# Whole K loads, w_out's remainder in four transfers, and mask copies on GpSimd in a decode step bound by its cache reads

## The chip, the cores and the metric

The kernel runs on one core of one Trainium2 chip. The core has five engines with instruction streams of their own: TensorE (PE; its weight loads are listed as PEld), VectorE (DVE), ScalarE (ACT), GpSimd (POOL) and SyncE (SP), which here only issues transfers. Sixteen DMA engines move data between the memory outside (HBM) and the on-chip SBUF. The metric is the device time of one execution in microseconds, as the median of several runs.

## The reference

One decode step of attention with a large cache, and a small gated MLP beside it, both on the layer-normed input (weights, caches and inputs in bfloat16):

```python
# x (4,1,640); k_cache, v_cache (4,32,4096,128); wq (640,4096); wo (4096,640)
# w_in (640,1728); w_sp (1,1); b_sp (1,); w_out (864,640)
xn = layernorm(x)
# A: attention of 4 x 32 heads, one query each
q = (xn @ wq) as (4,32,1,128)
p = softmax(q . k_cache * 128**-0.5)          # over 4096 keys
A = (p . v_cache) as (4,1,4096) @ wo
# B: gated MLP
z  = gelu_tanh(xn @ w_in)                     # (4,1,1728)
z2 = layernorm(z[..., 864:])
g  = w_sp * z2 + b_sp
B  = (z[..., :864] * g) @ w_out
out = x + A + B
```

Each cache holds 134 MB, and every byte of it is used once. The other weights come to some 14 MB.

## The kernel before

**Units and places.** The caches are cut into 16 units each: 4 groups g of 8 heads, times 4 batch rows b, with u = 4g + b. A unit is 8.39 MB, 65536 bytes on each of 128 partitions. The SBUF has five slots of half a unit; every load has a fixed pair of them. A K load of an odd unit goes to slots 2 and 3, of an even one to 3 and 4, and a V load mostly to 0 and 1. SyncE issues the loads in the order of `seq`, and each issue waits until the last reader of its slots is done.

```python
    seq = [("k", u) for u in range(B)]
    for u in range(NU):
        seq.append(("v", u))
        if u + B < NU:
            seq.append(("k", u + B))
    ...
    for u in range(B, NU):
        place[("k", u)] = (3, 4) if u % 2 == 0 else (2, 3)
    for u in range(NU):
        place[("v", u)] = (0, 1)
    place[("v", 0)] = (1, 2)
    place[("v", NU - 3)] = (2, 3)
    place[("v", NU - 1)] = (3, 4)
    cuts = {("k", u): (0, T // 2, T) for u in range(NU) if u % B == B - 1}
    cuts[("v", NU - 1)] = (0, 192, T)
    first = {u: u % 2 for u in range(B, NU) if ("k", u) not in cuts}
    ...
        for t0, t1 in zip(c[:-1], c[1:]):
            nc.sync.dma_start(out=unit(item, t0, t1), in_=src[:, t0 * Dh:t1 * Dh])
```

A load in `cuts` comes as two transfers, each with its own completion: the last K of each group (units 3, 7, 11 and 15). `first` says which half of a whole K load is read first, so that the slot which the next K load needs comes free early.

**K side.** A unit of K takes eight steps. In each, VectorE transposes 128 x 2048 words into one of two `kT` buffers, and TensorE multiplies that with the queries (QZ) into the scores S of the group.

```python
        hh = first.get(u, 0) ^ (k // 4)
        ...
        kT = ktpool.tile([P, NKT], F32, tag="kT", name="kT")[:, 0:2 * TC * 32]
        nc.vector.transpose(kT[:].rearrange("p (t r) -> p t r", r=32), kw)
        ...   # 8 matmuls of 128x512
```

After the group's fourth unit the softmax follows: maximum, exponent (ScalarE), a transpose, sixteen copies into `xd`, and then the masks for b = 0 and 1. `z_fill` writes the weights of TensorE's V side into one of two buffers Zb, each head masked by MkE:

```python
    def z_fill(g, b):
        xd = state[("xd", g)]
        for hp in range(HP):                  # 4
            ...
            for e in range(NE):               # 2
                dst = Zb[b % 2][r0:r0 + 32, :, NE * hp + e, :]
                mk = MkE[r0:r0 + 32, e:e + 1]
                if b == 0 and e == 0 and hp < 3:
                    nc.vector.tensor_scalar(out=dst, in0=src, scalar1=mk, scalar2=None, op0=ALU.mult)
                else:
                    nc.scalar.activation(out=dst, in_=src, func=ACT.Copy, scale=mk)
```

**V side.** A unit of V is 64 matmuls with Zb as weights. VectorE then masks and sums the result, and the masks for b + 2 are written.

```python
        for w in range(NW):
            q = w % 4
            nc.tensor.matmul(O_ps[32 * q:32 * q + 32, :, :], lhsT=Zb[b % 2][:, w].rearrange("p h c -> p (h c)"),
                             rhs=vv[:, w * 4 * Dh:(w + 1) * 4 * Dh], start=(w < 4), stop=(w >= NW - 4))
        ...
        if b + 2 < B:
            z_fill(g, b + 2)
```

**MLP.** Its 864 inner columns are 512 on all partitions (FA = 4 chunks) and a remainder of 352, laid out as 44 partitions x 8 chunks. `w_rest` holds the rows of w_out for the remainder and borrows one of the two `kT` buffers before the first K unit needs it:

```python
    w_rest_t = ktpool.tile([P, NKT], F32, tag="kT", name="w_rest")
    w_rest = w_rest_t[:NRP].bitcast(BF16)[:, 0:FR * NOUT].rearrange("p (c n) -> p c n", c=FR)
    r_at = [nf, nf + FR * RP[0], Fh]
    for i in range(2):
        nc.sync.dma_start(out=w_rest[32 * i:32 * i + RP[i]].rearrange("p c n -> p (c n)"),
                          in_=B_w_out[r_at[i]:r_at[i + 1], :].rearrange("(r i c) n -> i r (c n)", r=4, c=FR))
```

The first transfer has i = 8 by r = 4 rows of 10240 bytes, the second i = 3 by r = 4.

Of the kernel before, what the change touches and what calls it, by code (L numbers as in the profile page):

```python
# [9 lines left out]
ALU = mybir.AluOpType  # L10
AX = mybir.AxisListType
F32 = mybir.dt.float32
BF16 = mybir.dt.bfloat16
# [3 lines left out]
def kernel(  # L17
# [19 lines left out]
    nc = tc.nc  # L37
    P = 128
    B, Sq, D = A_x.shape
    _, H, Sk, Dh = A_k_cache.shape  # L40
    assert Sq == 1 and B == 4 and Dh == P and D % P == 0
    DC = D // P
# [4 lines left out]
    T = Sk // M  # L47
    C2 = 2
    TC = 32
# [3 lines left out]
    NU = NG * B  # L53
    G = HG * B
    F2 = B_w_in.shape[1]
    Fh = F2 // 2
    FA = 4
    FR = 8
    RI = (8, 3)
    RP = [4 * i for i in RI]  # L60
    NRP = sum(RP)
    assert Fh == FA * P + FR * NRP and RP[0] == 32
    FC = FA + FR
    NOUT = A_wo.shape[1]
    NH = 2
    NO2 = NOUT // NH
# [3 lines left out]
    const = ctx.enter_context(tc.tile_pool(name="const", bufs=1))  # L70
    small = ctx.enter_context(tc.tile_pool(name="small", bufs=2))

    NKT = max(2 * TC * 32, FR * NOUT // 2)
    ktpool = ctx.enter_context(tc.tile_pool(name="ktpool", bufs=2))
    ppool = ctx.enter_context(tc.tile_pool(name="ppool", bufs=3))
    ps_s = ctx.enter_context(tc.tile_pool(name="ps_s", bufs=1, space=bass.MemoryType.PSUM))
# [7 lines left out]
    def misc_ps(shape, dtype):  # L84
        misc_ctr[0] += 1
        return ps_m.tile(shape, dtype, tag="misc", name=f"misc{misc_ctr[0]}")
# [5 lines left out]
    def at_slot(i, n, off=0):  # L92
        return kv[:, i * SL + off:i * SL + off + n]
# [24 lines left out]
    nf = FA * P  # L118
    w_out = at_slot(2, FA * NOUT, n_in).rearrange("p (c n) -> p c n", c=FA)
    nc.sync.dma_start(out=w_out, in_=B_w_out[0:nf, :].rearrange("(p c) n -> p c n", p=P))  # L120
    w_rest_t = ktpool.tile([P, NKT], F32, tag="kT", name="w_rest")
    w_rest = w_rest_t[:NRP].bitcast(BF16)[:, 0:FR * NOUT].rearrange("p (c n) -> p c n", c=FR)
    r_at = [nf, nf + FR * RP[0], Fh]
    for i in range(2):
        nc.sync.dma_start(out=w_rest[32 * i:32 * i + RP[i]].rearrange("p c n -> p (c n)"),  # L125
                          in_=B_w_out[r_at[i]:r_at[i + 1], :].rearrange("(r i c) n -> i r (c n)", r=4, c=FR))

    NB = 32 * FC
    z_at = n_in + FA * NOUT
# [12 lines left out]
    place[("v", 0)] = (1, 2)  # L142
    place[("v", NU - 3)] = (2, 3)
    place[("v", NU - 1)] = (3, 4)
    cuts = {("k", u): (0, T // 2, T) for u in range(NU) if u % B == B - 1}
    cuts[("v", NU - 1)] = (0, 192, T)
    first = {u: u % 2 for u in range(B, NU) if ("k", u) not in cuts}

    def unit(item, t0, t1):

        s0, s1 = place[item]
        assert s1 == s0 + 1 or t1 <= T // 2 or t0 >= T // 2
        if t0 >= T // 2:
            return at_slot(s1, (t1 - t0) * Dh, t0 * Dh - SL)
        return at_slot(s0, (t1 - t0) * Dh, t0 * Dh)
# [50 lines left out]
    xnT = const.tile([P, DC, 32], BF16)  # L206
# [67 lines left out]
    for hf in range(2):  # L274
        for c in range(DC):
            for j in range(NG):
                n0 = j * HG * Dh + hf * 512
                nc.tensor.matmul(q4_ps[32 * j:32 * j + 32, hf * 512:hf * 512 + 512], lhsT=xnT[:, c, :],  # L278
                                 rhs=wq[:, c, n0:n0 + 512], start=(c == 0), stop=(c == DC - 1))
# [13 lines left out]

    w_z = w_in.rearrange("p c (a f) -> p c a f", a=2)
    z_ps = misc_ps([P, 2, FA, 32], F32)
    zr_ps = misc_ps([64, 2, FR * 32], F32)
    w_za = w_z[:, :, :, 0:nf].rearrange("p c a (q j i) -> p c q a i j", q=4, j=32)
    for c in range(DC):
        for q in range(4):
            nc.tensor.matmul(z_ps[32 * q:32 * q + 32], lhsT=xnT[:, c, :], rhs=w_za[:, c, q], start=(c == 0), stop=(c == DC - 1))  # L300
        for i in range(2):
            nc.tensor.matmul(zr_ps[32 * i:32 * i + 32, :, 0:FR * RP[i]], lhsT=xnT[:, c, :],
                             rhs=w_z[:, c, :, r_at[i]:r_at[i + 1]], start=(c == 0), stop=(c == DC - 1))
    z_f = at_slot(2, 2 * 3 * NB, z_at).bitcast(F32).rearrange("p (a n) -> p a n", a=3)
    z_b = at_slot(2, 2 * NB, z_at + 6 * NB).rearrange("p (a n) -> p a n", a=2)
    zT = z_f[:, 0:2, :].rearrange("p a (i j) -> p a i j", j=32)
    nc.gpsimd.memset(z_f[:, 0:2, :], 0.0)
    nc.scalar.activation(out=zT[:, :, 0:FA, :], in_=z_ps[:], func=ACT.Gelu_apprx_tanh)
    for i in range(2):
        for a in range(2):  # L310
            nc.scalar.activation(out=zT[32 * i:32 * i + 32, a, FA:FC, 0:RP[i]].rearrange("p c (i r) -> p c i r", r=4),
                                 in_=zr_ps[32 * i:32 * i + 32, a, 0:FR * RP[i]].rearrange("p (r i c) -> p c i r", r=4, c=FR),
                                 func=ACT.Gelu_apprx_tanh)

    one_bf = const.tile([1, P], BF16)
# [19 lines left out]
                                   op0=ALU.mult, op1=ALU.subtract)  # L335
# [14 lines left out]
    for fc in range(FC):  # L350
        n = P if fc < FA else NRP
        nb = B if fc > 1 else 32
        r0 = 64 * (fc % 2)
        for hf in range(NH):
            nc.tensor.matmul(proj[r0 + 32 * hf:r0 + 32 * hf + nb, 0:NO2], lhsT=uT[:n, fc, 0:nb],
                             rhs=(w_out[:, fc] if fc < FA else w_rest[:, fc - FA])[:, hf * NO2:(hf + 1) * NO2], start=(fc < 2), stop=False)


    def fill_qz(g):
# [8 lines left out]
    def emit_K(u, k):  # L368
# [5 lines left out]
        kw = unit(("k", u), t0, t0 + 2 * TC).bitcast(F32).rearrange("p (t w) -> p t w", w=KW)[:, :, 32 * kh:32 * kh + 32]  # L374
        kT = ktpool.tile([P, NKT], F32, tag="kT", name="kT")[:, 0:2 * TC * 32]
        nc.vector.transpose(kT[:].rearrange("p (t r) -> p t r", r=32), kw)  # L376
# [34 lines left out]
    def z_fill(g, b):  # L411
        xd = state[("xd", g)]
        for hp in range(HP):
            r0 = 32 * hp
            src = xd[r0:r0 + 32, C2 * b:C2 * b + C2].rearrange("p x q (y c) -> p (x q y) c", c=4)
            for e in range(NE):
                dst = Zb[b % 2][r0:r0 + 32, :, NE * hp + e, :]
                mk = MkE[r0:r0 + 32, e:e + 1]
                if b == 0 and e == 0 and hp < 3:
                    nc.vector.tensor_scalar(out=dst, in0=src, scalar1=mk, scalar2=None, op0=ALU.mult)  # L420
                else:
                    nc.scalar.activation(out=dst, in_=src, func=ACT.Copy, scale=mk)  # L422

    def softmax(g):
        negmax = softmax_max(g)
        S_ps = state.pop(("S", g))
        p_bf = ppool.tile([P, TC, NE, M], BF16, tag="p", name="p")
        rowsum = small.tile([P, NE], F32, tag="rowsum")
        for e in range(NE):
            nc.scalar.activation(out=p_bf[:, :, e, :], in_=S_ps[:, e], func=ACT.Exp, bias=negmax[:, e:e + 1], scale=scale,  # L430
                                 accum_out=rowsum[:, e:e + 1])

        pT = ppool.tile([P, TC, HP, B * C2], BF16, tag="p", name="pT")
        nc.vector.transpose(pT[:].rearrange("p t h x -> p (t h x)"), p_bf[:].rearrange("p t e m -> p (t e m)"))  # L434

        xd = small.tile([P, B * C2, 4, TC], BF16, tag="xd", name="xd", bufs=1)
        state[("xd", g)] = xd
        for hp in range(HP):
            for q in range(4):
                op = nc.vector.tensor_copy if q < 2 or (hp < 3 and q == 2) else nc.scalar.copy  # L440
                op(out=xd[32 * hp:32 * hp + 32, :, q, :], in_=pT[32 * q:32 * q + 32, :, hp, :].rearrange("p t x -> p x t"))  # L441
        z_fill(g, 0)
        z_fill(g, 1)
        rs8 = small.tile([P, NE, B], F32, tag="rs8")
        nc.gpsimd.tensor_tensor(out=rs8[:], in0=rowsum[:, :, None].to_broadcast((P, NE, B)),  # L445
                                in1=MkB[:, None, :].to_broadcast((P, NE, B)), op=ALU.mult)
        cs = misc_ps([P, B], F32)
        for e in range(NE):
            nc.tensor.matmul(cs[:], lhsT=SelE[:, e].rearrange("p h e q -> p (h e q)"), rhs=rs8[:, e, :],  # L449
                             start=(e == 0), stop=(e == NE - 1))  # L450
        rinv = small.tile([P, B], F32, tag="rinv")
        nc.vector.reciprocal(out=rinv[:], in_=cs[:])
        state[("rinv", g)] = rinv
# [56 lines left out]
    for i, item in enumerate(seq):  # L510
        if i + 1 < len(seq):
            key, u = seq[i + 1]
# [10 lines left out]
        key, u = item  # L523
        g, b = divmod(u, B)
# [31 lines left out]
    for c in range(HG):  # L556

        p = part.get(c, 0)
        lhsT = oT[:, c, :] if p in seen else oT[:, c:c + HG, :].rearrange("p c b -> p (c b)")
        nb = B if p in seen else 32  # L560
        for hf in range(NH):
            nc.tensor.matmul(last[p][32 * hf:32 * hf + nb, :], lhsT=lhsT,  # L562
                             rhs=wo_t[NG - 1][:, c, hf * NO2:(hf + 1) * NO2], start=p not in seen, stop=c in (5, HG - 1))
# [36 lines left out]
```

## Time and profile before

| | |
|---|---|
| time, median of 3 runs | 663.5 us (663.31 to 663.76) |
| span of the profiled execution | 661.7 us |
| DVE busy | 362.1 us (55%), 282.8 of it in the K transposes (L376, 128 of 2276 ns) |
| PE busy | 289.6 us (44%) |
| ACT busy | 78.8 us (12%), 52.9 of it in 116 mask copies (L422, 498 ns each) |
| POOL busy | 21.1 us (3%) |
| read from HBM | 282.25 MB, mean 427 GB/s over the span |

The page's numbered parts are the busy time of the engines, the span in 40 slices of 16.5 us each (a digit is the busy share in tenths), the DMA queues, the chain of work that ended last, the costliest groups of instructions and the transfers. L376 and the like are lines of the kernel. Engine names with a q at the end (SPq) stand for that engine's issuing part. A line of the timeline gives the start, the duration, the engine, the line and operation, the tiles written and read with their shapes, the number of instructions in a row, and in brackets the idle time before them with what ended it. The trace also has each DMA packet with its start, duration and size, but not the number of its DMA engine. A transfer over all sixteen DMA engines reports sixteen completions, one for each engine; where they come apart, the engines are at different points of the same queue.

### The profile page before, as it was taken

To read this page: it belongs to the slowest core of one execution; us is meant where nothing else is said; L and a number is where in the kernel's file an instruction comes from. 1 tells how busy PE (TensorE), PEld (TensorE's weight loads), DVE (VectorE), ACT (ScalarE), POOL (GpSimd) and SP (SyncE) were. 2 spreads that over 40 slices of the span, in tenths; PEclk is the share of its full clock that TensorE was granted. 3 is DMA by queue.
4 is the path that set the end of the run, shared out by engine and by line. 5 is a ranking of instruction groups with operands and counts; after the bars stand their busy time and mean duration, and the time that the engine had idled before them with its cause. 6 is when DMAs were issued, how large, how long until landed. Compare 5 with 4: busy or idle time off the path is not lost.

```text
span 661.7 us, 5325 instructions
## 1 busy us (share of the span) xinstructions
PE 289.6 (44%) x2246; PEld 105.5 (16%) x2246; DVE 362.1 (55%) x279; ACT 78.8 (12%) x165; POOL 21.1 (3%) x66
## 2 busy tenths in 40 slices
PE   0425655356072455224436065533707255533235
PEld 0101111112021122111112021110202112111112
DVE  2238999656191759619256286745529175961113
ACT  0300000430100000530200000070020000053200
POOL 6300000000000000000000000000000000000000
PEclk9859979779577687677758587765767758766677
DMA  9999999999999999999999999999999999999996
GB/s 373 450 445 420 424 447 442 420 445 421 436 433 436 428 419 451 421 436 445 436 420 437 420 425 450 443 428 433 416 444 433 440 425 418 435 444 426 427 423 273
DMA packets 6891, 282.59 MB, mean 427 GB/s; under 512 B 787, under 2 KB 1063, under 8 KB 1447
## 3 DMA queue, kind: packets, MB, share of 16 engines
q1 hardware_dynamic: 6847, 282.25, 98.9%
q8 instruction: 17, 0.28, 0.2%
q14 instruction: 7, 0.06, 0.0%
q10 hardware_dynamic: 20, 0.01, 0.0%
HBM read 282.25 MB, written 0.01 MB: 427 GB/s over the span
## 4 chain that ended last, share of the span: by engine, by line
DMA 73%; DVE 11%; issue 11%; PE 2%; ACT 1%; SPq 1%; DVEq 0%; ACTq 0%
DMA kv<-in_A_k_cache_dram 65%; DVE kT L376 11%; DMA kv<-in_A_v_cache_dram 5%; DMA kv<-in_A_wo_dram 3%; PE O L461 1%; ACT Zb L422 0%; ACT xd L441 0%; SPq L125 0%; ACT p L430 0%; DVE pT L434 0%; PE last_a L562 0%; DVE m L394 0%; PE S L387 0%; SPq L172 0%; PE misc L399 0%
## 5 line engine op out<-in xcount | busy, mean ns | idle before, releaser
L376 DVE STREAM_TRANSPOSE kT<-kv 128x2048 f32<-128x2048 f32 x128 | 282.8, 2276 | 121.8 <-DMA kv<-in_A_k_cache_dram 121.7
L387 PE MATMUL S<-kT,QZ 128*32 128x512 bf16 x1024 | 188.0, 500 | 256.7 <-DVE kT L376 256.7
L387 PEld LDWEIGHTS <-QZ 128*32 128x32 bf16 x1024 | 60.0, 110 | 382.6 <-issue 323.5
L461 PE MATMUL O<-kv,Zb 128*32 128x512 bf16 x1024 | 76.7, 466 | 59.0 <-DMA kv<-in_A_v_cache_dram 41.9
L470 DVE TENSOR_TENSOR om<-O,Mk 128x512 f32<-128x512 f32 x15 | 10.4, 692 | 111.2 <-PE O L461 111.2
L422 ACT ACTIVATE Zb<-xd,MkE 32x256 bf16<-32x256 bf16 x116 | 52.9, 498 | 113.5 <-PE O L461 112.1
L430 ACT ACTIVATE p<-S,negmax 128x512 bf16<-128x512 f32 x8 | 5.4, 683 | 400.0 <-DVE negmax L408 400.0
L461 PEld LDWEIGHTS <-Zb 128*32 128x32 bf16 x1024 | 33.7, 115 | 102.8 <-issue 66.3
L362 POOL COPY QZ<-qT 32x32 bf16<-32x32 bf16 x16 | 5.1, 317 | 383.3 <-PE S L387 382.7
L441 DVE COPY xd<-pT 32x256 bf16<-32x256 bf16 x44 | 15.9, 361 | 0.8
L471 DVE TENSOR_REDUCE R<-om 128x128 f32<-128x512 f32 x15 | 15.3, 1019 | 0.5
L441 ACT COPY xd<-pT 32x256 bf16<-32x256 bf16 x20 | 12.3, 613 | 5.6 <-DVE pT L434 5.2
L449 PE MATMUL misc<-rs,SelE 128*128 128x4 f32 x16 | 4.1, 359 | 11.4 <-POOL rs L445 8.5
L434 DVE STREAM_TRANSPOSE pT<-p 128x1024 bf16<-128x1024 bf16 x4 | 5.0, 1245 | 6.3 <-ACT p L430 6.3
L473 DVE TENSOR_SCALAR R<-O,Mk 128x128 f32<-128x128 f32 x1 | 0.4, 351 | 14.0 <-PE O L461 14.0
L278 PE MATMUL q<-kv,xnT 128*32 128x512 bf16 x40 | 4.5, 630 | 7.6 <-DMA kv<-in_A_wq_dram 7.6
L483 PE MATMUL misc<-R,SelX 128*128 128x512 f32 x8 | 4.5, 644 | 7.2 <-DVE R L471 5.5
L394 DVE TENSOR_REDUCE m<-S 128x2 f32<-128x1024 f32 x4 | 4.9, 1225 | 4.9 <-PE S L387 4.9
L286 DVE CAST kv<-q 128x512 bf16<-128x512 f32 x1 | 0.7, 692 | 11.8 <-PE q L278 11.8
L399 PE MATMUL misc<-dg,ones_f 128*128 128x256 f32 x8 | 3.1, 474 | 7.2 <-DVE dg L396 7.2
L445 POOL TENSOR_TENSOR rs<-rowsum,MkB 128x8 f32<-128x8 f32 x4 | 0.8, 201 | 166.4 <-ACT p L430 166.4
L449 PEld LDWEIGHTS misc<-rs,SelE 128*128 128x128 f32 x16 | 3.7, 322 | 13.3 <-POOL rs L445 9.7
(103 smaller groups left out, 76.1 us busy)
## 6 DMA issues: line engine op xcount, KB each, us to landing
kv<-in_A_k_cache_dram SPq DMA_DIRECT2D x8, 4096.0 KB, 29.8
kv<-in_A_v_cache_dram SPq DMA_DIRECT2D x1, 6144.0 KB
kv<-in_A_wq_dram SPq DMA_DIRECT2D x1, 5120.0 KB, 15.1
kv<-in_A_wo_dram SPq DMA_DIRECT2D x3, 1280.0 KB, 21.5
kv<-in_B_w_in_dram SPq DMA_DIRECT2D x1, 2160.0 KB
kv<-in_A_v_cache_dram SPq DMA_DIRECT2D x1, 2048.0 KB
kv<-in_B_w_out_dram SPq DMA_DIRECT2D x1, 640.0 KB, 20.8
kv<-in_A_wo_dram SPq DMA_DIRECT2D x1, 640.0 KB
```

The source lines that it names most:

```text
L362: nc.gpsimd.tensor_copy(out=QZ[r0:r0 + 32, :, :, :, 8 + 8 * hp], in_=qT[32 * g:32 * g + 32, NE * hp:NE * hp + NE].rearrange("p e a b -> p ...
L376: nc.vector.transpose(kT[:].rearrange("p (t r) -> p t r", r=32), kw)
L387: nc.tensor.matmul(S_ps[32 * q:32 * q + 32, e], lhsT=QZ[:, b, 2 * kh + w, e, w0:w0 + 32], rhs=kb[:, i, :, e, :, w], start=(b == 0 and k < ...
L394: nc.vector.tensor_reduce(out=m1[:], in_=S_ps[:].rearrange("p e t m -> p e (t m)"), axis=AX.X, op=ALU.max)
L422: nc.scalar.activation(out=dst, in_=src, func=ACT.Copy, scale=mk)
L430: nc.scalar.activation(out=p_bf[:, :, e, :], in_=S_ps[:, e], func=ACT.Exp, bias=negmax[:, e:e + 1], scale=scale, accum_out=rowsum[:, e:e + 1])
L434: nc.vector.transpose(pT[:].rearrange("p t h x -> p (t h x)"), p_bf[:].rearrange("p t e m -> p (t e m)"))
L441: op(out=xd[32 * hp:32 * hp + 32, :, q, :], in_=pT[32 * q:32 * q + 32, :, hp, :].rearrange("p t x -> p x t"))
L449: nc.tensor.matmul(cs[:], lhsT=SelE[:, e].rearrange("p h e q -> p (h e q)"), rhs=rs8[:, e, :], start=(e == 0), stop=(e == NE - 1))
L461: nc.tensor.matmul(O_ps[32 * q:32 * q + 32, :, :], lhsT=Zb[b % 2][:, w].rearrange("p h c -> p (h c)"), rhs=vv[:, w * 4 * Dh:(w + 1) * 4 * ...
L470: nc.vector.tensor_tensor(out=om4[:], in0=O_ps[:], in1=Mk4[:, :, None].to_broadcast((P, 4, Dh)), op=ALU.mult)
L471: nc.vector.tensor_reduce(out=R, in_=om4[:].rearrange("p c d -> p d c"), axis=AX.X, op=ALU.add)
```

## The change

It has three parts:

- The last K loads of the second and third group (units 7 and 11) come whole. Their halves are then read in the order that `first` gives: slot 3 first, which the next K load needs. The last K loads of the first and the fourth group (units 3 and 15) stay cut in two. This makes for fewer transfers with longer rows.
- The remainder of w_out is laid out as 44 partitions x 9 chunks, of which the last two are partly filled: four transfers of 8 x 4 rows of 8960 bytes, 5 x 4 of 1280, 3 x 4 of 8960 and 3 x 4 of 2560. Seven chunks lie in one `kT` buffer and two in the other, so both are borrowed, and the `kT` buffers shrink from 10240 to 8960 bytes per partition. GpSimd clears the second buffer first. The GELU of the remainder comes in eight pieces instead of four.
- For b = 2 and 3, half of the mask copies (hp = 2 and 3, four of eight) go to GpSimd: 32 of the 128 copies, which relieves ScalarE.

The order of instructions on TensorE and VectorE is otherwise kept: in both kernels the selection and sum of the group before (L486 to L494) stand ahead of the eight transposes of the group's last K unit.

```diff
@@ -55,11 +55,10 @@
     F2 = B_w_in.shape[1]
     Fh = F2 // 2
     FA = 4
-    FR = 8
-    RI = (8, 3)
-    RP = [4 * i for i in RI]
-    NRP = sum(RP)
-    assert Fh == FA * P + FR * NRP and RP[0] == 32
+    FR = 9
+    RB = ((0, 0, 8, 7), (0, 7, 5, 1), (1, 0, 3, 7), (1, 7, 3, 2))
+    NRP = 44
+    assert Fh == FA * P + 4 * sum(i * c for _, _, i, c in RB)
     FC = FA + FR
     NOUT = A_wo.shape[1]
     NH = 2
@@ -70,7 +69,7 @@
     const = ctx.enter_context(tc.tile_pool(name="const", bufs=1))
     small = ctx.enter_context(tc.tile_pool(name="small", bufs=2))
 
-    NKT = max(2 * TC * 32, FR * NOUT // 2)
+    NKT = max(2 * TC * 32, 7 * NOUT // 2)
     ktpool = ctx.enter_context(tc.tile_pool(name="ktpool", bufs=2))
     ppool = ctx.enter_context(tc.tile_pool(name="ppool", bufs=3))
     ps_s = ctx.enter_context(tc.tile_pool(name="ps_s", bufs=1, space=bass.MemoryType.PSUM))
@@ -118,12 +117,17 @@
     nf = FA * P
     w_out = at_slot(2, FA * NOUT, n_in).rearrange("p (c n) -> p c n", c=FA)
     nc.sync.dma_start(out=w_out, in_=B_w_out[0:nf, :].rearrange("(p c) n -> p c n", p=P))
-    w_rest_t = ktpool.tile([P, NKT], F32, tag="kT", name="w_rest")
-    w_rest = w_rest_t[:NRP].bitcast(BF16)[:, 0:FR * NOUT].rearrange("p (c n) -> p c n", c=FR)
-    r_at = [nf, nf + FR * RP[0], Fh]
-    for i in range(2):
-        nc.sync.dma_start(out=w_rest[32 * i:32 * i + RP[i]].rearrange("p c n -> p (c n)"),
-                          in_=B_w_out[r_at[i]:r_at[i + 1], :].rearrange("(r i c) n -> i r (c n)", r=4, c=FR))
+    w_rest = []
+    for k, n in ((0, 7), (1, 2)):
+        t = ktpool.tile([P, NKT], F32, tag="kT", name=f"w_rest{k}")[:NRP].bitcast(BF16)[:, 0:n * NOUT]
+        w_rest.append(t.rearrange("p (c n) -> p c n", c=n))
+    nc.gpsimd.memset(w_rest[1].rearrange("p c n -> p (c n)").bitcast(F32), 0.0)
+    r_at = [nf]
+    for q, c0, ni, n in RB:
+        r_at.append(r_at[-1] + 4 * ni * n)
+        k = c0 // 7
+        nc.sync.dma_start(out=w_rest[k][32 * q:32 * q + 4 * ni, 0:n].rearrange("p c n -> p (c n)"),
+                          in_=B_w_out[r_at[-2]:r_at[-1], :].rearrange("(r i c) n -> i r (c n)", r=4, c=n))
 
     NB = 32 * FC
     z_at = n_in + FA * NOUT
@@ -142,7 +146,7 @@
     place[("v", 0)] = (1, 2)
     place[("v", NU - 3)] = (2, 3)
     place[("v", NU - 1)] = (3, 4)
-    cuts = {("k", u): (0, T // 2, T) for u in range(NU) if u % B == B - 1}
+    cuts = {("k", u): (0, T // 2, T) for u in (B - 1, NU - 1)}
     cuts[("v", NU - 1)] = (0, 192, T)
     first = {u: u % 2 for u in range(B, NU) if ("k", u) not in cuts}
 
@@ -293,23 +297,25 @@
 
     w_z = w_in.rearrange("p c (a f) -> p c a f", a=2)
     z_ps = misc_ps([P, 2, FA, 32], F32)
-    zr_ps = misc_ps([64, 2, FR * 32], F32)
+    zr_ps = misc_ps([64, 2, 256], F32)
     w_za = w_z[:, :, :, 0:nf].rearrange("p c a (q j i) -> p c q a i j", q=4, j=32)
     for c in range(DC):
         for q in range(4):
             nc.tensor.matmul(z_ps[32 * q:32 * q + 32], lhsT=xnT[:, c, :], rhs=w_za[:, c, q], start=(c == 0), stop=(c == DC - 1))
-        for i in range(2):
-            nc.tensor.matmul(zr_ps[32 * i:32 * i + 32, :, 0:FR * RP[i]], lhsT=xnT[:, c, :],
-                             rhs=w_z[:, c, :, r_at[i]:r_at[i + 1]], start=(c == 0), stop=(c == DC - 1))
+        for q in range(2):
+            f0, f1 = r_at[2 * q], r_at[2 * q + 2]
+            nc.tensor.matmul(zr_ps[32 * q:32 * q + 32, :, 0:f1 - f0], lhsT=xnT[:, c, :],
+                             rhs=w_z[:, c, :, f0:f1], start=(c == 0), stop=(c == DC - 1))
     z_f = at_slot(2, 2 * 3 * NB, z_at).bitcast(F32).rearrange("p (a n) -> p a n", a=3)
     z_b = at_slot(2, 2 * NB, z_at + 6 * NB).rearrange("p (a n) -> p a n", a=2)
     zT = z_f[:, 0:2, :].rearrange("p a (i j) -> p a i j", j=32)
     nc.gpsimd.memset(z_f[:, 0:2, :], 0.0)
     nc.scalar.activation(out=zT[:, :, 0:FA, :], in_=z_ps[:], func=ACT.Gelu_apprx_tanh)
-    for i in range(2):
+    for (q, c0, ni, n), f0, f1 in zip(RB, r_at[:-1], r_at[1:]):
+        f0, f1 = f0 - r_at[2 * q], f1 - r_at[2 * q]
         for a in range(2):
-            nc.scalar.activation(out=zT[32 * i:32 * i + 32, a, FA:FC, 0:RP[i]].rearrange("p c (i r) -> p c i r", r=4),
-                                 in_=zr_ps[32 * i:32 * i + 32, a, 0:FR * RP[i]].rearrange("p (r i c) -> p c i r", r=4, c=FR),
+            nc.scalar.activation(out=zT[32 * q:32 * q + 32, a, FA + c0:FA + c0 + n, 0:4 * ni].rearrange("p c (i r) -> p c i r", r=4),
+                                 in_=zr_ps[32 * q:32 * q + 32, a, f0:f1].rearrange("p (r i c) -> p c i r", r=4, c=n),
                                  func=ACT.Gelu_apprx_tanh)
 
     one_bf = const.tile([1, P], BF16)
@@ -353,7 +359,7 @@
         r0 = 64 * (fc % 2)
         for hf in range(NH):
             nc.tensor.matmul(proj[r0 + 32 * hf:r0 + 32 * hf + nb, 0:NO2], lhsT=uT[:n, fc, 0:nb],
-                             rhs=(w_out[:, fc] if fc < FA else w_rest[:, fc - FA])[:, hf * NO2:(hf + 1) * NO2], start=(fc < 2), stop=False)
+                             rhs=(w_out[:, fc] if fc < FA else w_rest[(fc - FA) // 7][:, (fc - FA) % 7])[:, hf * NO2:(hf + 1) * NO2], start=(fc < 2), stop=False)
 
 
     def fill_qz(g):
@@ -418,6 +424,8 @@
                 mk = MkE[r0:r0 + 32, e:e + 1]
                 if b == 0 and e == 0 and hp < 3:
                     nc.vector.tensor_scalar(out=dst, in0=src, scalar1=mk, scalar2=None, op0=ALU.mult)
+                elif b > 1 and hp > 1:
+                    nc.gpsimd.tensor_scalar(out=dst, in0=src, scalar1=mk, scalar2=None, op0=ALU.mult)
                 else:
                     nc.scalar.activation(out=dst, in_=src, func=ACT.Copy, scale=mk)
```

## The prediction

> **What bounds the kernel now.** I read the page's slices first, then the DMA queues, then the chain that ended last, and only then the engines.
>
> ```profile
> DMA  9999999999999999999999999999999999999996
> GB/s 373 450 445 420 424 447 442 420 445 421 436 433 436 428 419 451 421 436 445 436 420 437 420 425 450 443 428 433 416 444 433 440 425 418 435 444 426 427 423 273
> ...
> q1 hardware_dynamic: 6847, 282.25, 98.9%
> ...
> DMA 73%; DVE 11%; issue 11%; PE 2%; ACT 1%; SPq 1%; DVEq 0%; ACTq 0%
> ```
>
> All but the last slice have the DMA engines at nine tenths or more, and SyncE's queue fills 98.9% of sixteen engines' span. No compute engine passes 55%. So the time is 282 MB at the engines' own rate, plus the head, the tail and any bubble; an edit counts only if it alters (a) the time of the packets, (b) their spread over the sixteen engines, or (c) lets an engine run dry because a load was issued too late. In the packet records a 65536-byte packet takes 2424 ns (27.0 GB/s an engine, 433 GB/s for sixteen), a 32768-byte one 1217.6 ns. The chain's 11% of VectorE is hidden time: each DMA link in it lasts about 29.8 us although 8.39 MB needs 19.4; the rest is queueing behind the load before.
>
> For (c) I looked for the load with the least lead over the end of the load before it, near the change. Issues on SyncE's queue around the third group's last K load (start, us, line, operation, tiles):
>
> ```profile
> 362.59 23.50 SPq L164 DMA_DIRECT2D kv<-in_A_k_cache_dram  x2
> 399.97 0.33 SPq L164 DMA_DIRECT2D kv<-in_A_v_cache_dram  x1
> 424.63 0.33 SPq L164 DMA_DIRECT2D kv<-in_A_k_cache_dram  x1
> 443.41 0.33 SPq L164 DMA_DIRECT2D kv<-in_A_v_cache_dram  x1
> ```
>
> Call the loads K11 (two halves, issued at 362.59 and 385.76 by the chain), V8, K12, V9. VectorE's timeline shows what V9 waits for, first on the way to the softmax:
>
> ```profile
> 405.90 8.89 DVE L376 STREAM_TRANSPOSE kT<-kv 128x2048 f32<-128x2048 f32 x4 [0.93 <-DMA kv<-in_A_k_cache_dram]
> 415.71 8.89 DVE L376 STREAM_TRANSPOSE kT<-kv 128x2048 f32<-128x2048 f32 x4 [0.92 <-DMA kv<-in_A_k_cache_dram]
> 425.82 1.23 DVE L394 TENSOR_REDUCE m<-S 128x2 f32<-128x1024 f32 x1 [1.22 <-PE S L387]
> ...
> 436.79 0.89 DVE L420 TENSOR_SCALAR Zb<-xd,MkE 32x256 bf16<-32x256 bf16 x3
> 443.41 0.69 DVE L470 TENSOR_TENSOR om<-O,Mk 128x512 f32<-128x512 f32 x1 [5.73 <-PE O L461]
> ```
>
> and TensorE's timeline the last step:
>
> ```profile
> 438.08 5.28 PE L461 MATMUL O<-kv,Zb 128*32 128x512 bf16 x64 [5.61 <-ACT Zb L422]
> ```
>
> K11's second half lands at 415.59; four transposes, softmax and the first masks take until 438.08; the 64 matmuls on V8 free V8's place at 443.41, and V9 is issued that instant. From landing to issue: 27.82 us. K12 lands at 454.31.
>
> [...] The old w_rest transfers have i = 8 and i = 3 outermost, [...] K0, right behind them, finishes its sixteen shares in three clusters, 7 within 0.93 us of the first, 6 at 1.51 to 1.86, 3 at 3.04 to 3.31; rows of 387.5 ns make 1.55 and 3.10 us for four and eight. [...] here the first packet of the wq load starts 1.0 us after its issue (0.73 to 1.74), and I use 1.0. [...]
>
> **The change part by part.**
>
> *Whole K loads (K7, K11), packet time.* Each engine trades 32 packets of 32768 bytes for 16 of 65536: 32 x 1217.6 - 16 x 2424.2 = 176 ns. Minus 0.18 us.
>
> *Whole K loads, issue.* A whole K11 needs both places, so it goes out when the first half went free last: 385.76, as its second half does now. V7 is then still loading until 392.2 on its fastest engine (packet records): lead 6 us, no bubble. K7 likewise: 227.71 against 234.1.
>
> *Whole K loads, the softmax.* All eight transposes now follow the landing. K12's eight take
>
> ```profile
> 454.33 17.66 DVE L376 STREAM_TRANSPOSE kT<-kv 128x2048 f32<-128x2048 f32 x8 [9.17 <-DMA kv<-in_A_k_cache_dram]
> ```
>
> on VectorE, so the softmax comes 8.8 to 8.9 us later. The selection and sum of the group before stand ahead of the transposes in program order and stay hidden. V9's issue moves to 443.41 + 8.89 = 452.3, first packet 453.3. The sixteen engines finish K12 staggered: seven between 450.3 and 451.9, nine between 453.2 and 453.8. The fast seven idle 1.4 to 3 us, the slow nine 0 to 0.1. The end is set by the slow ones, whose lag grows to the end (spread 4.6 us from 474 on), so a pause of the fast engines costs nothing. I charge +0.1.
>
> In the second group V4's own landing (its matmuls start at 280.10) was the last wait, V5 moves from 285.89 to about 294.2, first packet 295.2, and K8's shares end between 295.4 and 298.95, later by the w_o load in between: no bubble, +0.
>
> *w_out's rest.* [...] A 1280-byte packet takes 55 ns, a 2560-byte one 103, 5120 takes 196 and 10240 takes 387.5, so 8960 is about 340. The three most loaded engines go from 8 x 387.5 = 3.10 us to 4 x (340 + 55 + 340 + 103) = 3.35: plus 0.25 us on the engines that end last. The longer head of that branch (four more small GELU pieces, some 0.65 us from 358 ns for 256 columns and 234 for 96; two more matmuls) ends near 36.3 instead of 35.4; the first transpose needs the buffers at 44.2. Two more issues of 0.85 us delay K0's from 4.02 to 5.8, with queued work until 20. Hidden.
>
> *Masks on GpSimd.* 32 of ScalarE's 116 copies of 498 ns leave it, 16 us of ScalarE in all. A GpSimd tensor_scalar of 384 f32 columns took 666 and 1658 ns, so 256 columns at 0.45 to 1.1 us, four in a row 1.8 to 4.4 us, against 3.68 us for eight on ScalarE. They fill masks for b = 2 and 3, used a whole V load (19 us or more) later. Worth 0, in the last group too: the mask for V14 is filled by about 604 and V14 lands at 629.67.
>
> Sum: 663.5 - 0.18 + 0.10 + 0.25 = 663.7.
>
> **The rivals.**
>
> *Starvation at V9 reaches the slow engines.* For: the estimated margin is -0.1 to +0.5 us, thinner than the uncertainty of the first-packet latency (at the start the engines' first packets came 1.0 to 2.1 us after issue) and of the 64 matmuls (5.28 to 5.96 us here). Against: only the part beyond 453.2 counts. At 2.1 us latency, +1.1: about 664.8. Were the selection's 2 us pushed behind the landing too, +2 more: 666.5; the program order speaks against it.
>
> *Balance instead of loss.* The four transfers could spread evenly over sixteen engines. Then the three slow engines lose 3.1 - 1.1 = 2 us of lag; other lags (single idle gaps of about 1 us in the records) would keep most engines where they are, and the end might come 0.5 to 1 us earlier: 662.8. [...]
>
> *GpSimd in VectorE's way.* A copy that overlaps K12's transposes could hold them; K13's load has over 9 us of lead, so even 4 us would vanish: 663.7 still.
>
> **Range and chances.** The sum is 0.2 us above before. Down: no bubble and no extra lag, 663.3, and the runs' own scatter of 0.25. Up: 1.1 for a late first packet. So 663.0 to 664.9 eight times in ten. Two per cent is 13.3 us, and only a bubble at every load could make that: within 2% at 0.97, slower 0.02, faster 0.01.
>
> **What would show it.** K11 issued once near 385.8; eight transposes in a row after its landing; V9's issue near 452.3 and a dip of DMA share just before 454; V5 near 294; K0's shares ending with three engines about 3.35 us behind the first; GpSimd near 40 us busy, ScalarE near 63, VectorE unchanged. Wrong would be: V9 issued after 453.5, K8 or K12's slowest share followed by an idle DMA of over 1 us, a smaller spread at K0, or a pause at any other load.

## The result, and the profile after

The changed kernel takes 666.04 us (median of 6 runs, 665.47 to 668.09) against 663.74 for the kernel before on the same chips: a ratio of 1.0040, 95% interval 1.0024 to 1.0056. It is 2.3 us slower, where 0.2 was expected and 664.9 us was the upper end. The profiled execution after took 667.36 us, 1.3 more than the median. Its last microsecond is not to be explained by the change: the packet records show a single engine that paused for 1.0 us at 563.9 and then took 1.71 us for a packet that usually takes 1.22, and from there on the last share of each load comes some 1.5 us later.

The page of the changed kernel, for comparison with the first fence of the prediction:

```profile
DMA  9999999999999999999999999999999999999995
GB/s 370 448 442 441 417 436 437 430 426 438 437 438 429 425 434 425 438 418 430 433 434 429 433 434 437 430 433 375 441 437 435 429 411 428 451 425 435 420 425 243
...
q1 hardware_dynamic: 6599, 282.25, 98.5%
...
DMA 71%; DVE 12%; issue 11%; PE 3%; ACT 1%; SPq 0%; POOL 0%; DVEq 0%; ACTq 0%
```

The bytes are the same and still everything hangs on the DMA engines. One slice stands out: the 28th, from 449 to 466 us, with 375 GB/s, where before had 433. The line of busy tenths hides it. Five per cent of a slice is 0.8 us, and a packet that takes longer than usual still counts as busy.

SyncE's issues there (start, us):

```profile
386.46 0.33 SPq L168 DMA_DIRECT2D kv<-in_A_k_cache_dram  x1
400.67 0.33 SPq L168 DMA_DIRECT2D kv<-in_A_v_cache_dram  x1
425.15 0.33 SPq L168 DMA_DIRECT2D kv<-in_A_k_cache_dram  x1
452.96 0.33 SPq L168 DMA_DIRECT2D kv<-in_A_v_cache_dram  x1
```

K11 now goes out once, at 386.46, and K12 keeps its time. V9 goes out at 452.96 instead of 443.41, while K12 ends 0.8 us later than before. VectorE's timeline and TensorE's say why, as foretold:

```profile
416.23 17.66 DVE L382 STREAM_TRANSPOSE kT<-kv 128x2048 f32<-128x2048 f32 x8 [10.56 <-DMA kv<-in_A_k_cache_dram]
435.10 1.22 DVE L400 TENSOR_REDUCE m<-S 128x2 f32<-128x1024 f32 x1 [1.21 <-PE S L393]
```

```profile
447.06 5.85 PE L469 MATMUL O<-kv,Zb 128*32 128x512 bf16 x64 [5.66 <-ACT Zb L430]
```

Eight transposes follow the landing at 416.21, and the softmax with its masks reaches TensorE at 447.06. From landing to V9's issue it is 36.75 us; the prediction had 27.82 + 8.89 = 36.71.

Two stretches of 15 us of before, then the same two of after. The columns are the stretch and its length, the busy us of PE, PEld, DVE, ACT and POOL with the number of instructions, the granted PE clock, the DMA share and GB/s; a packet counts where it starts:

```profile
435.00:450.00 15.00, 5.28 (x64) 2.01 (x64) 4.23 (x10) 10.14 (x22) 0.00 (x0) 0.73 0.97 419
450.00:465.00 15.00, 7.40 (x32) 2.11 (x33) 10.67 (x5) 0.00 (x0) 0.00 (x0) 0.50 0.99 425
```

```profile
435.00:450.00 15.00, 4.71 (x36) 2.32 (x38) 8.60 (x21) 9.81 (x21) 1.47 (x5) 0.60 1.01 437
450.00:465.00 15.00, 8.76 (x72) 2.85 (x65) 11.58 (x7) 2.53 (x6) 3.68 (x4) 0.72 0.95 386
```

Between 450 and 465 the changed kernel moves 0.59 MB less, which is 1.4 us of transfer. The packet records show how. K12's sixteen shares end from 451.80 to 454.66. Fourteen of the sixteen engines had nothing left to do when V9's first packet came. Thirteen start on V9 between 453.93 and 454.28, 1.0 to 1.3 us after its issue, one at 454.71, and two only at 456.20 and 456.84. In the mean an engine was idle for 1.2 us. All sixteen first packets take 2.78 to 3.38 us instead of 2.42, 0.7 us more in the mean. V9's last share then ends 22.17 us after K12's last; 19.35 us is what a unit needs (eight packets of 2.42 us an engine).

### The profile page after: what moved, and what is told of

Read it like the earlier page. It is cut to its first block, busy times and chain, and to the rows that moved or that the text cites. A ratio compares the mean times of both kernels' runs of the same rounds, so it can differ in the third digit from the quotient of the medians.

```text
span 665.6 us, 5346 instructions
## 1 busy us (share of the span) xinstructions
PE 290.0 (44%) x2248; PEld 105.7 (16%) x2248; DVE 362.2 (54%) x279; ACT 64.6 (10%) x137; POOL 51.4 (8%) x99
## 4 chain that ended last, share of the span: by engine, by line
DMA 71%; DVE 12%; issue 11%; PE 3%; ACT 1%; SPq 0%; POOL 0%; DVEq 0%; ACTq 0%
DMA kv<-in_A_k_cache_dram 61%; DVE kT L382 11%; DMA kv<-in_A_v_cache_dram 5%; DMA kv<-in_A_wo_dram 3%; DMA kv<-in_A_wq_dram 2%; PE O L469 2%; PE q L282 1%; PE S L393 0%; ACT xd L449 0%; ACT Zb L430 0%; SPq L176 0%; ACT p L438 0%; DVE pT L442 0%; DVE kv L291 0%; DVE m L400 0%
## 5 line engine op out<-in xcount | busy, mean ns | idle before, releaser
L469 PE MATMUL O<-kv,Zb 128*32 128x512 bf16 x1024 | 78.3, 474 | 63.0 <-DMA kv<-in_A_v_cache_dram 39.9
L430 ACT ACTIVATE Zb<-xd,MkE 32x256 bf16<-32x256 bf16 x84 | 38.6, 499 | 105.0 <-PE O L469 104.0
L428 POOL TENSOR_SCALAR Zb<-xd,MkE 32x256 bf16<-32x256 bf16 x32 | 29.4, 920 | 139.6 <-PE O L469 137.4
```

Of the source, the lines that this page charges most:

```text
L428: nc.gpsimd.tensor_scalar(out=dst, in0=src, scalar1=mk, scalar2=None, op0=ALU.mult)
```

## The experiments

The theory: a whole K load makes a later V load late; the DMA engines run dry together, and the restart costs more than the idle time itself. The rivals: the four w_out transfers, the masks on GpSimd, or whole K loads by themselves (longer transfers, later release of their slots).

**First round: one part at a time.**

`a1_k_cut_again` undoes the first part in the changed kernel:

```diff
-    cuts = {("k", u): (0, T // 2, T) for u in (B - 1, NU - 1)}
+    cuts = {("k", u): (0, T // 2, T) for u in range(NU) if u % B == B - 1}
```

> The changed kernel with units 7 and 11 of K cut in two again; the four w_out transfers and the masks on GpSimd stay. Starvation theory (the late V loads after the two whole K loads cost the 2.3 us): V9 is issued about 11 us before K12 ends, no engine runs dry, 663.6 to 664.2. Rival w_out (uneven rows and the 12 us wait of its fourth transfer): stays at 665.5 to 666. Rival masks (GpSimd in the way): stays at 665.5 to 666.

Measured: 663.88 us, ratio to before 1.0000 (0.9992 to 1.0008). The loss is gone, with both other parts still in.

`a2_k_whole_only` is the kernel before with the reverse edit:

> The kernel before with units 7 and 11 of K whole, nothing else. Starvation theory: nearly the whole loss is here, 665.3 to 666.1, with two bubbles as in the changed kernel (V5's about 0.7 us on the slowest engine, V9's about 1.8). Rival w_out and rival masks: 663.5, the packets' 0.18 us less than before.

Measured: 665.55 us, 1.0028 (1.0016 to 1.0040). Most of the loss by this part alone.

`a3_wout_only` is the changed kernel with the old `cuts` and without the mask branch (the `elif b > 1 and hp > 1` and its line removed):

> The kernel before with only the four w_out transfers (and the smaller kT buffers that come with them). Starvation theory: 663.7 to 664.1, 0.25 us for the three most loaded DMA engines at most. Rival w_out: 665.5 or more.

Measured: 664.14 us, 1.0004 (0.9996 to 1.0012): not told apart from zero; the expected 0.25 us lies inside.

`a4_masks_only` is the kernel before with that branch:

> The kernel before with only the 32 mask copies on GpSimd. Starvation theory: 663.7 as before within 0.2, since those masks are ready a whole V load early. Rival masks: 664.5 or more.

Measured: 663.77 us, 0.9997 (0.9989 to 1.0005): nothing. The three parts alone add up to 0.0028 + 0.0004 - 0.0003 = 0.0029 of the 0.0040, within their intervals.

**Second round: which load, and is it the lateness.**

`b1_k11_whole` and `b2_k7_whole` are the kernel before with one of the two K loads whole:

```diff
-    cuts = {("k", u): (0, T // 2, T) for u in range(NU) if u % B == B - 1}
+    cuts = {("k", u): (0, T // 2, T) for u in (3, 7, 15)}     # b1: K11 whole
+    cuts = {("k", u): (0, T // 2, T) for u in (3, 11, 15)}    # b2: K7 whole
```

> The kernel before with only K11 (third group) whole. Starvation with a costly restart: V9 is issued about 1.5 us before K12's slowest share ends, all sixteen DMA engines restart, first packets of about 3.1 us instead of 2.42 and one or two engines 2 us late; K12 to V9, last landing to last landing, 21.5 to 22.2 us instead of 19.35; time 664.9 to 665.7, most of the loss of both loads together (665.55). Rival, whole loads cost by themselves (longer transfers, later slot release, PE clock): half of the loss here, half in the next run, 664.6 in both.

Measured: 665.32 us, 1.0021 (1.0012 to 1.0029).

> The kernel before with only K7 (second group) whole. Starvation: V5 has 3 us of lead over K8's slowest share thanks to the w_o load in between, so part of the engines restart and the slowest loses 0.7 us or less; time 663.8 to 664.5. Rival, whole loads cost by themselves: 664.6.

Measured: 664.26 us, 1.0005 (0.9997 to 1.0013). So most of the loss sits at K11, and the same edit at K7 can't be told from nothing. The rival that each whole load costs the same asked for 664.6 twice; that value lies at the edge of both intervals, but the runs themselves are apart: b1's twelve from 664.79 to 666.30, b2's thirteen from 663.39 to 665.09. SyncE's issue of V9 in b1, and the stretch of 450 to 465 us:

```profile
453.74 0.33 SPq L164 DMA_DIRECT2D kv<-in_A_v_cache_dram  x1
```

```profile
450.00:465.00 15.00, 9.75 (x70) 3.15 (x65) 11.22 (x7) 4.42 (x10) 0.00 (x0) 0.67 0.83 338
```

V9 was issued here at 453.74 (the 64 matmuls before it took 6.53 us); in b2 it was 444.95. All sixteen engines were done with K12 at 454.07 and started from 454.69 to 455.55, after 1.9 us of idle time in the mean. The second late load of after, V5, tells why K7 does little: the w_o load between K7 and V4 delays K8's end by 3 us, and when the first packet of V5, issued at 295.50, comes at 296.54, thirteen of the sixteen engines are still at work. Eight of V5's first packets took 2.72 to 3.24 us, but the load lost only 0.65 us in the mean.

`b3_v5_v9_cut` keeps both whole K loads in the changed kernel and gives V5 and V9 an earlier start:

```diff
     cuts[("v", NU - 1)] = (0, 192, T)
+    cuts[("v", B + 1)] = cuts[("v", 2 * B + 1)] = (0, T // 2, T)
```

> The changed kernel with V5 and V9 cut in two halves, K7 and K11 still whole. The first half's place is free when half of the 64 matmuls are done, so its issue comes nearly 3 us earlier (about T + 33.8 after K11 lands instead of T + 36.7). Starvation: the slow engines find work, no restart on them, 663.7 to 664.4. Rival, whole loads cost by themselves: stays at 665.5 to 666.

Measured: 664.40 us, 1.0006 (0.9997 to 1.0014). SyncE's issue of V9 in this kernel, both halves in one line:

```profile
450.56 2.06 SPq L169 DMA_DIRECT2D kv<-in_A_v_cache_dram  x2
```

and its stretch of 450 to 465 us, with 407 GB/s where after has 386:

```profile
450.00:465.00 15.00, 8.00 (x72) 2.65 (x65) 12.19 (x7) 2.58 (x6) 3.68 (x4) 0.88 0.96 407
```

The same whole K loads, the same late softmax, and once V9's first half goes out at 450.56, 2.4 us sooner, all but 0.7 us of the loss is gone, and that rest is within the interval. V9's last share ends 19.42 us after K12's last. Six engines reached it early: three of them had to wait, for 0.1 to 1.0 us, and the first packets of all six, of 32768 bytes, took 1.39 to 1.94 us instead of 1.22. The ten that were longer at K12 went on without a loss. This is the run that separates lateness from whole loads as such.

`b5_k15_whole` is the kernel before with the last group's K15 whole (`cuts` for 3, 7 and 11), where two V loads become late:

> The kernel before with only K15 (the last group's last unit) whole, a larger dose: V13 waits for all of K15's transposes and V14 for the softmax that comes 8.9 us later. Starvation: two restarts (V13 issued near 589.5 against V12's last share at 590.4, V14 near 609 to 610), 2 to 5 us more than before: 666 to 669. Rival, whole loads cost by themselves: about 664.6 as for one load.

Measured: 666.14 us, 1.0035 (1.0022 to 1.0048). V13 was issued at 589.46 and V14 at 608.13. One restart came, at V13. The second did not: V14's issue was 2.2 us ahead of the first end of V13, and V14 lost 0.14 us in the mean. The stretch before the restart, in the kernel before and then in b5 with the stretch that follows:

```profile
575.00:590.00 15.00, 6.46 (x34) 2.62 (x30) 11.11 (x15) 3.31 (x8) 0.20 (x1) 0.73 1.01 437
```

```profile
575.00:590.00 15.00, 10.37 (x60) 3.34 (x58) 14.43 (x7) 0.00 (x0) 0.00 (x0) 0.77 0.82 355
590.00:605.00 15.00, 4.74 (x32) 2.27 (x32) 8.59 (x21) 8.81 (x19) 0.20 (x1) 0.57 1.02 419
```

The 355 GB/s stand where before has 437. V12's shares ended from 586.20 to 590.58, and all sixteen engines restarted between 590.41 and 590.83 with first packets of 2.85 to 3.54 us: the last engine waited at most 0.25 us. Yet fifteen shares of V13 ended by 610.98, 20.40 us after V12's last, which is 1.05 late, and the sixteenth's completion only came at 611.73, after a pause of 1.0 us of that one engine. In the mean V13 lost 2.64 us. So even an engine that hardly waits loses 0.4 to 1.1 us by its first packet; how the whole 2.4 us comes about is open.

The losses at V9 in one table, from the packet records (share of an engine = its part of a load; loss = end of V9's share less end of K12's less 19.35 us, by the last engine and as a mean over the sixteen sorted ends):

| kernel | V9 issued | K12's shares end | loss, last | loss, mean |
|---|---|---|---|---|
| before | 443.41 | 450.31 to 453.83 | 1.09 | 0.10 |
| a1 | 445.13 | 451.05 to 454.19 | 0.87 | 0.10 |
| b3 (first half) | 450.56 | 450.95 to 454.03 | 0.07 | 0.42 |
| after | 452.96 | 451.80 to 454.66 | 2.82 | 2.27 |
| b1 | 453.74 | 451.52 to 454.06 | 2.79 | 2.69 |
| a2 | 454.00 | 452.80 to 454.87 | 2.31 | 2.16 |

The 1.09 and 0.87 of before and a1 are a single engine that paused there; the mean shows that no restart took place. V5 loses 0.65 us in the mean in after, 0.56 in a2 and 0.21 in b2. The mean is no measure of the time: b1 and a2 lost 1.6 and 1.7 us in all, less than their means at V9. The packet records don't number the engines, so they don't tell which engine's delay reaches the end.

**Third round: a better kernel?** The spread of the sixteen engines starts at w_out's remainder: in before its transfers of 32 and 12 rows reported 8 and 3 completions, and K0's shares behind them ended up to 3.31 us apart. So I tried to even it out; how far another order of the rows would do so was my estimate. `c1_even_rows`:

```diff
-                          in_=B_w_out[r_at[i]:r_at[i + 1], :].rearrange("(r i c) n -> i r (c n)", r=4, c=FR))
+                          in_=B_w_out[r_at[i]:r_at[i + 1], :].rearrange("(p c) n -> p (c n)", c=FR))
...
-            ...zT[..., FA:FC, 0:RP[i]].rearrange("p c (i r) -> p c i r", r=4),
-                in_=zr_ps[...].rearrange("p (r i c) -> p c i r", r=4, c=FR),
+            ...zT[..., FA:FC, 0:RP[i]],
+                in_=zr_ps[...].rearrange("p (j c) -> p c j", c=FR),
```

> The kernel before with w_out's 32 + 12 remaining rows of 10240 bytes ordered so that the row index is the outermost dimension on both sides (8 consecutive rows of w_out per partition, no r by i order). [...] K0's sixteen shares then end within about 1 us of each other. If that lag reaches the end, 662.0 to 663.0; if single pauses of the engines make up the lag anyway, or the order by r was needed for the rate, 663.5 or more.

Measured: 666.70 us, 1.0034 (1.0022 to 1.0047): 3 us slower, a plain miss. The stretch of 20 to 30 us, before and then c1:

```profile
20.00:30.00 10.00, 3.42 (x37) 1.70 (x32) 3.69 (x8) 5.71 (x10) 3.20 (x8) 0.92 1.10 473
```

```profile
20.00:30.00 10.00, 3.58 (x41) 2.06 (x33) 3.68 (x8) 5.30 (x10) 2.78 (x8) 0.85 1.15 411
```

More busy and fewer bytes. In the packet records the 44 packets of 10240 bytes take 682 ns in the mean (up to 1053) where before has 385 for each, and K0's first packets on all sixteen engines take 2.5 to 4.2 us instead of 2.42. Together that is 13 + 17 = 30 us of engine time, 1.9 us for each of sixteen, of the 3 us measured; the rest is not accounted for. K0's shares do end closer together (1.9 us apart instead of 3.3), but all of them late.

`c2_even_rows_whole_k` puts the whole K7 and K11 and the cut V5 and V9 on top of c1:

> The kernel of even rows (before it, the kernel before) with K7 and K11 whole as in the change, and V5 and V9 cut in two against the starvation. The packets save 0.18 us and cost 0.09 back per cut V unit; no restart: same as the even rows alone within 0.4 us. If whole K loads cost by themselves: 1 us or more slower than the even rows.

Measured: 666.54 us, 1.0032 (1.0020 to 1.0044): the same as c1. Whole K loads cost nothing that shows when the V loads behind them are cut; their 0.18 us of packets is too small to be seen. "No restart" was not quite what came: V9's first half went out 0.37 us before K12's first share ended, some engines ran dry, and V9 lost 1.10 us in the mean and 0.44 on the last share.

`c3_even_rows_v1_cut` adds `cuts[("v", 1)] = (0, T // 2, T)` to c1:

> The kernel of even rows with V1 cut in two. V1 has the thinnest lead of the kernel before (issued 2.4 us before K4's first share ends, first packets of 2.6 to 2.9 us there). Its first half can go out some 3 us earlier. Starvation theory: 0 to 0.7 us faster than the even rows alone, as only the fast engines run dry there; the rival that the lead does not matter: 0.1 us slower for the smaller packets.

Measured: 666.83 us, 1.0038 (1.0025 to 1.0051): the same as c1. V1's thin lead costs nothing that shows here; in c1 it was 3.3 us, and V1 lost nothing there.

`d1_one_transfer` goes back to groups of four rows, in one transfer:

```diff
-    for i in range(2):
-        nc.sync.dma_start(out=w_rest[32 * i:32 * i + RP[i]]...,
-                          in_=B_w_out[r_at[i]:r_at[i + 1], :].rearrange("(r i c) n -> i r (c n)", r=4, c=FR))
+    nc.sync.dma_start(out=w_rest.rearrange("p c n -> p (c n)"),
+                      in_=B_w_out[nf:Fh, :].rearrange("(r i c) n -> i r (c n)", r=4, c=FR))
...      # the matmuls into zr_ps take the matching columns of w_in
-                             rhs=w_z[:, c, :, r_at[i]:r_at[i + 1]],
+                             rhs=w_zr[:, c, :, :, 64 * i:64 * i + FR * RI[i]],
```

> The kernel before with the 44 remaining rows of w_out in one transfer of i = 11 by r = 4 (row index (r, i, c) over all 352 rows): [...] Theory places: [...] at most 24 of the 44 packets near 770 ns, the other 20 at 385, K0's first packets at 2.42 us; time 663.3 to 664.3. Rival, order of rows: fewer than eight rows in a row on the three engines is all it takes, all 44 packets at 385 ns, largest lag at K0 1.6 us, 662.3 to 663.5. Rival, all engines in step: w_rest packets slow on all eleven engines and K0's first ones at 3 us or more, 665 or more.

Measured: 665.37 us, 1.0025 (1.0018 to 1.0032). 18 of the 44 packets took over 600 ns, where the theory of places had at most 24 near 770. That theory was my estimate, and no run shows what it supposes. K0's first packets took 2.6 to 3.8 us on all sixteen engines, where it had 2.42. The rival of engines in step foresaw them (its eleven engines are an estimate from before, where i = 8 and i = 3 came with 8 and 3 completions), but it also wanted all 44 packets slow. Neither holds alone, and the cause stays open. The time lost does go with the long packets: they hold 7.5 + 15 us of engine time more than usual here, 1.4 us for each of sixteen, for 1.6 us measured.

None of the twelve runs beats the kernel before.

## Why the prediction was wrong, point by point

**What bounds the kernel, and the lateness: right.** DMA all along; K11 issued once (385.8 foretold, 386.46 measured), eight transposes in a row, V9's issue at 36.75 us after K11's landing (36.71 foretold), its first packets 1.0 us after the start of the issue, as it was reckoned. The issuing instruction itself takes 0.33 us, so from its end it is 0.64. In absolute time V9 came at 452.96 instead of 452.3.

**The step that failed: the price of that lateness.** The prediction let the seven engines that are ahead idle 1.4 to 3 us and the nine that set the end 0 to 0.1, held the idle time of the seven to be free and the first packets to be as fast as any, and concluded: "I charge +0.1." It should have charged about 2: V9's last share came 2.82 us late in after (1.09 in before), and 2.27 in the mean (0.10 in before). Three things were mis-sized.

- The idle time. By the prediction's own figures it is some 0.8 us in the mean over sixteen engines (an estimate, from K12's ends in before and a first packet at 453.3). It was 1.2 in after, 1.4 in a2 and 1.9 in b1. Part of it are stragglers: engines that start 2 to 3 us behind the others in after, and one or two in a2 and b1 half a microsecond to a microsecond behind. Why they straggle is open.
- The first packet. It took some 3.1 us instead of 2.42 (on all 16 engines in after, 14 in b1, 15 in a2), 0.7 us more in the mean in each of the three, and the prediction had nothing for it. In b5 the last engine waited at most 0.25 us, and V13 was still 1.05 us late, the paused engine left out.
- The margin. It was taken to a tenth of a microsecond against a group of 64 matmuls whose time varies: 5.12 us in b3, 5.85 in after and 6.53 in b1, with a granted PE clock of 0.98, 0.84 and 0.69 from 450 to 455 us. In b1 and a2 V9's issue came late enough for the last engine to be idle too.

That a pause of the fast engines alone costs nothing is not refuted: in b3 three engines waited, V9's last share lost 0.07 us, and what is left of the loss can't be told from nothing.

The mechanism stood in the prediction as its first rival, "Starvation at V9 reaches the slow engines", with the right place and too small a price (664.8; the 666.5 that it also names needed another order of instructions, which did not come). The runs that settle it are b1 against b2 (place) and b3 (cure).

**V5, +0: right in time, not in the reason.** K7 alone adds nothing that can be measured. But "no bubble" did not hold: V5 was issued at 295.50 instead of 294.2, three engines were out of work before its first packet came, and the load lost 0.65 us in the mean in after.

**Packets, -0.18: not visible**, as it had to be: the runs of before in the first round alone go from 663.36 to 665.30 us. c2 against c1 has 0.16 us with the right sign and no weight.

**w_out, +0.25: consistent.** The four transfers, with 8, 5, 3 and 3 outermost, reported 8, 5, 3 and 3 completions, as the two of before, with 8 and 3, reported 8 and 3. K0's shares in after end with three engines 3.11 to 3.47 us behind the first (3.35 foretold; 3.04 to 3.31 in before). That the same three engines carry rows of all four transfers was my estimate, which these times fit; the records don't name the engine. Alone, 1.0004 with zero and the expected 0.25 us both inside the interval. One thing was missed without harm: the fourth of these transfers was issued only at 16.12, just after the wq load had landed at 16.11, and K0 after it at 16.89 (5.8 foretold). The queue held work until 20 us.

**Masks, 0: right.** The ratio alone was 0.9997, with 1 inside the interval. The copies took longer than the estimate's middle, 920 ns each, so GpSimd was busy for 51.4 us and not 40:

```profile
L428 POOL TENSOR_SCALAR Zb<-xd,MkE 32x256 bf16<-32x256 bf16 x32 | 29.4, 920 | 139.6 <-PE O L469 137.4
```

Four in a row take 3.95 us, from 453.10 to 457.05 beside K12's transposes, which kept their 17.66 us for eight: no sign that GpSimd holds VectorE up. Before the run, that there would be no delay was my estimate.

**The rival of balance was wrong in a way worth having:** the four transfers did not spread evenly (8, 5, 3 and 3 completions), and where evening out the rows was tried, in c1 and d1, the packets were slower instead (682 and 555 ns in the mean, 385 in before).

## What to carry to other kernels

In a kernel that its transfers bound, look at the lead of each load's issue over the first engine's end of the load before, and at what an edit takes from it: here merging two half loads saved 0.18 us of packets and used up 9 us of lead where only 7 to 10 were there. Do not price a queue that runs dry at the idle time of the slowest engine. Where fourteen or more engines ran dry here (V9 in after, a2 and b1, V13 in b5), the load came 2.2 to 2.7 us late in the mean and the kernel lost 1.6 to 2.4; where fewer did (V5 in after, a2 and b2, V9 in b3), the load lost 0.2 to 0.7 us in the mean, and the two kernels with nothing else, b2 and b3, lost 0.5 and 0.7, which can't be told from nothing. When a load has to be late, cut it so that its first half depends on half of the work: in b3 that gave back all but 0.7 us of the loss without undoing the edit.

## What the runs showed of the hardware that was not expected

- After a restart the DMA engines' first packets of 65536 bytes took mostly 2.8 to 3.5 us instead of 2.42, and the second ones 2.42 again (2.42 to 2.71 at V9 in after). It takes neither all sixteen in step nor a long wait: at V5 in after eight first packets took 2.72 to 3.24 us while other engines were still at K8, and at V9 in b3 six took 1.39 to 1.94 us instead of 1.22 for half the size, three of them on engines that had not waited for even 0.1 us. On the other hand two stragglers, at 455.55 us in b1 and 455.77 in a2, took the usual time. What makes the first packet slow is not shown.
- The order of 44 rows, 0.45 MB in all, went with 1.6 to 3 us: in before, where 32 of them came with 8 completions and 12 with 3, a row took 385 ns, in the two other orders 555 (d1) and 682 (c1) in the mean, and K0's first packets were slow too (2.6 to 3.8 us in d1, 2.5 to 4.2 in c1, 2.42 in before). The records don't name the engine of a packet, and why the order matters is not shown.
